# Two edits to a state-space and PReLU kernel: the last output blocks turned by TensorE, and a copy of the first group moved

## Chip, cores, metric

The kernel runs on one core of a Trainium2 chip. The metric is device time in microseconds (us), taken from repeated executions; a profile of one execution comes with it.

Names in the profile: PE is TensorE (PEld its weight loads), DVE is VectorE, ACT is ScalarE, POOL is GpSimd, SP is SyncE, which here only issues transfers and waits; a q behind a name is that engine's instruction queue. PSUM is the memory, in banks, that takes TensorE's products. A semaphore is a counter on which an engine waits.

## The reference, cut to what matters

```python
# x (4,8,768,32), a (4,8,768), B and C (4,8,768,16): a state-space layer, in chunks of 32
y = ssd(x, a, B, C)                          # state decays by a, output C . state
h = y.transpose(0, 2, 1, 3).reshape(3072, 256)
g = h @ w_in                                 # 256 -> 2048
g = max(g, 0) + alpha * min(g, 0)            # a slope per hidden unit
out = g @ w_out                              # 2048 -> 256, all in fp32
```

## The kernel before, the parts concerned

The 3072 tokens go in six groups of 512. Group 0 has plain products. The other groups use a scheme of seven products of half-size blocks in place of eight (as in Strassen's method), so that sums on VectorE and GpSimd, and copies on ScalarE, stand for one product in eight on TensorE. The seven results of a group lie in half banks of PSUM. From them `combine` makes two blocks `c[0]` and `c[1]` of 128 output columns by 512 tokens. They stand the wrong way round (columns on partitions), so `turn` turns them in 32x32 blocks on VectorE and stores pieces of 32 columns.

```python
def output(f, half=None):                    # group 0, second matrix
    ...
    if f == NF - 1 and half:                 # the last product of group 0
        for i, po in enumerate(pos.pop(0)):
            o_sb = op.tile([P, 2, d_model], F32, name="o_sb")
            nc.scalar.copy(out=o_sb, in_=po)             # L543
            nc.sync.dma_start(out=out[...], in_=o_sb)    # L545

HALVES = {1: (0, 0), 2: (0, 1), 7: (1, 0), 6: (1, 1), 3: (2, 0), 4: (2, 1), 5: (3, 0)}
#         product: (bank, half)

def combine(g):                              # cut; the branches of the last group
    nc.scalar.copy(out=sa[:, 0], in_=m[1])
    nc.vector.tensor_tensor(out=c[0][:, 0], in0=m[2], in1=sa[:, 0], op=ALU.add)
    turn(g, 0, c[0], slice(0, HT), engs)
    nc.scalar.copy(out=sa[:, 1], in_=m[5])
    nc.vector.tensor_tensor(out=u[:, 0], in0=m[6], in1=sa[:, 0], op=ALU.add)      # L687
    nc.vector.tensor_tensor(out=u[:, 1], in0=m[7], in1=u[:, 0], op=ALU.add)
    nc.vector.tensor_tensor(out=u[:, 0], in0=u[:, 0], in1=sa[:, 1], op=ALU.add)   # L690
    nc.gpsimd.tensor_tensor(out=c[1][:, 1], in0=u[:, 1], in1=sa[:, 1], op=ALU.add)
    nc.vector.tensor_tensor(out=c[1][:, 0], in0=u[:, 1], in1=m[4], op=ALU.subtract)  # L693
    turn(g, 1, c[1], slice(0, GT), engs)
    nc.vector.tensor_tensor(out=c[0][:, 1], in0=m[3], in1=u[:, 0], op=ALU.add)
    turn(g, 0, c[0], slice(HT, GT), engs)

def turn(g, i, c, ts, engs):
    nc.vector.transpose(o[:, :n], c.rearrange("p h t -> p (h t)")[:, ts])   # 32x32 blocks
    for a4 in range(P // 32):                # four transfers, rows of 32 floats = 128 B
        engs[a4 % len(engs)].dma_start(out=..., in_=o[32 * a4 : 32 * a4 + 32, :n]...)

for n in (1, 2, 5, 6, 7, 4, 3):              # the very end: the seven last products,
    product(NG - 1, NZ - 1, n)
for _ in combine(NG - 1):                    # then everything else
    pass
```

Of the kernel before, what the change touches and what calls it, by code (L numbers as in the profile page):

```python
# [9 lines left out]
F32 = mybir.dt.float32  # L10
U32 = mybir.dt.uint32
U16 = mybir.dt.uint16
ALU = mybir.AluOpType
# [9 lines left out]
def kernel(  # L23
# [25 lines left out]
    nc = tc.nc  # L49
# [6 lines left out]
    P = 128  # L56
    Q = 128
# [5 lines left out]
    d_model, d_ff = moe_w_in.shape  # L63
    KC = d_model // P
    NF = d_ff // P
    GC = 4
    GT = GC * Q
    NG = NCH // GC
# [3 lines left out]
    NZ = NF // 4  # L72
    HM = d_model // 2
    HT = GT // 2
# [10 lines left out]
    wtp = ctx.enter_context(tc.tile_pool(name="wtp", bufs=2))  # L85
# [3 lines left out]
    one = ctx.enter_context(tc.tile_pool(name="one", bufs=1))  # L89
# [4 lines left out]
    op = ctx.enter_context(tc.tile_pool(name="op", bufs=3))  # L94
    dr = ctx.enter_context(tc.tile_pool(name="dr", bufs=1, space=bass.MemoryType.DRAM))
    ps_s = ctx.enter_context(tc.tile_pool(name="ps_s", bufs=2, space=PSUM))
    ps_h = ctx.enter_context(tc.tile_pool(name="ps_h", bufs=2, space=PSUM))
    ps_q = ctx.enter_context(tc.tile_pool(name="ps_q", bufs=1, space=PSUM))

    def bank(i):  # L100


        return ps_q.tile([P, 512], F32, name="bank", tag=f"q{i}")
# [104 lines left out]
    def convert(dst, src, sg, add=nc.gpsimd):  # L208
# [14 lines left out]
        else:  # L223
            for i in range(2):
# [8 lines left out]
    ident = const.tile([P, P], F32, name="ident")  # L233
# [3 lines left out]
                          in_=ident.unsqueeze(1).to_broadcast([P, H, Q]))  # L237
# [275 lines left out]
    pos = {}  # L513
# [17 lines left out]
    def output(f, half=None):  # L531

        if f == 0:
            pos[0] = [bank(i).rearrange("p (t m) -> p t m", t=2) for i in range(GC // 2)]
        gt = gts[0, f]
        for t in range(GC) if half is None else range(2 * half, 2 * half + 2):
            nc.tensor.matmul(pos[0][t // 2][:, t % 2], gt[:, t * Q : (t + 1) * Q], w_out[:, f],  # L537
                             start=(f == 0 and t % 2 == 0), stop=(f == NF - 1),
                             skip_group_check=True)
        if f == NF - 1 and half:  # L540
            for i, po in enumerate(pos.pop(0)):
                o_sb = op.tile([P, 2, d_model], F32, name="o_sb")
                nc.scalar.copy(out=o_sb, in_=po)  # L543
                t0 = 2 * i * Q
                nc.sync.dma_start(  # L545
                    out=out[t0 : t0 + 2 * Q, :].rearrange("(s p) m -> p s m", p=Q), in_=o_sb)



# [5 lines left out]
    def weight_sums(w, sums, q0, part):  # L555


        if not sums:
            sums.extend(wld.tile([P, NQ, P], F32, name=f"ws{i}", tag="raw") for i in range(3))
        qs = slice(q0, q0 + 4)  # L560
        a11, a12, a21, a22 = w[:, qs, 0, 0], w[:, qs, 0, 1], w[:, qs, 1, 0], w[:, qs, 1, 1]
        s1, s2, s4 = (t[:, qs] for t in sums)
        o, x0, x1, f = ((s1, a21, a22, ALU.add), (s2, s1, a11, ALU.subtract),
                        (s4, a12, s2, ALU.subtract), (a21, a11, a21, ALU.subtract))[part]
        nc.gpsimd.tensor_tensor(out=o, in0=x0, in1=x1, op=f)
# [13 lines left out]

    ms = {}  # L580
    HALVES = {1: (0, 0), 2: (0, 1), 7: (1, 0), 6: (1, 1), 3: (2, 0), 4: (2, 1), 5: (3, 0)}
    blocks = {}

    def product(g, z, n):

        if z == 0 and n == 1:
            ms[g] = [t.rearrange("p (h t) -> p h t", h=2)
                     for t in [bank(i) for i in range(3)] + m5_bank]
        i, h = HALVES[n]
        s1, s2, s4 = out_sums  # L590
        for p in range(2):
            q = 2 * z + p
            w = {1: wq[:, q, 0, 0], 2: wq[:, q, 1, 0], 3: s4[:, q], 4: wq[:, q, 1, 1],
                 5: s1[:, q], 6: s2[:, q], 7: wq[:, q, 0, 1]}[n]
            nc.tensor.matmul(ms[g][i][:, h], w, blocks[g, z][n][:, p],  # L595
                             start=(q == 0 and h == 0), stop=(q == NQ - 1),
                             skip_group_check=True)

    def prelu(o, h, z, i):
# [4 lines left out]
        for p in range(2):  # L604
            nc.vector.scalar_tensor_tensor(out=o[:, p], in0=h[:, p], scalar=s_mul[:, fs[p]],  # L605
                                           in1=o[:, p], op0=ALU.mult, op1=ALU.max)

    def quad(g, z, after):


# [58 lines left out]
    ends_of = {}  # L669

    def combine(g):


        m = {n: ms[g][i][:, h] for n, (i, h) in HALVES.items()}
        sa = wtp.tile([P, 2, HT], F32, name="sa", tag="wr")
        u = wtp.tile([P, 2, HT], F32, name="u", tag="wr")
        c = [one.tile([P, 2, HT], F32, name=f"c{i}") for i in range(2)]
        last = g == NG - 1
        engs = [nc.sync, nc.scalar]
        nc.scalar.copy(out=sa[:, 0], in_=m[1])  # L680
        nc.vector.tensor_tensor(out=c[0][:, 0], in0=m[2], in1=sa[:, 0], op=ALU.add)
        if last:
            turn(g, 0, c[0], slice(0, HT), engs)
        yield
        nc.scalar.copy(out=sa[:, 1], in_=m[5])
        yield
        nc.vector.tensor_tensor(out=u[:, 0], in0=m[6], in1=sa[:, 0], op=ALU.add)  # L687
        nc.vector.tensor_tensor(out=u[:, 1], in0=m[7], in1=u[:, 0], op=ALU.add)
        if last:
            nc.vector.tensor_tensor(out=u[:, 0], in0=u[:, 0], in1=sa[:, 1], op=ALU.add)  # L690
            nc.gpsimd.tensor_tensor(out=c[1][:, 1], in0=u[:, 1], in1=sa[:, 1], op=ALU.add)
        yield
        nc.vector.tensor_tensor(out=c[1][:, 0], in0=u[:, 1], in1=m[4], op=ALU.subtract)  # L693
        if last:
            turn(g, 1, c[1], slice(0, GT), engs)
        nc.vector.tensor_tensor(out=c[0][:, 1], in0=m[3], in1=u[:, 0], op=ALU.add)
        ms.pop(g)
        if last:
            turn(g, 0, c[0], slice(HT, GT), engs)
        else:  # L700
            nc.gpsimd.tensor_tensor(out=c[0][:, 1], in0=c[0][:, 1], in1=sa[:, 1], op=ALU.add)
            nc.gpsimd.tensor_tensor(out=c[1][:, 1], in0=u[:, 1], in1=sa[:, 1], op=ALU.add)
            ends_of[g] = c

    def turn(g, i, c, ts, engs):

        n = ts.stop - ts.start
        o = op.tile([P, GT], F32, name="o_sb")
        nc.vector.transpose(o[:, :n], c.rearrange("p h t -> p (h t)")[:, ts])
        for a4 in range(P // 32):  # L710
            m0 = i * HM + 32 * a4
            t0 = g * GT + ts.start
            engs[a4 % len(engs)].dma_start(
                out=out[t0 : t0 + n, m0 : m0 + 32].rearrange("(b r) c -> r b c", r=32),
                in_=o[32 * a4 : 32 * a4 + 32, :n].rearrange("r (b c) -> r b c", c=32))

    def finish(g, i):
        turn(g, i, ends_of[g][i], slice(0, GT), [nc.sync])
# [3 lines left out]
    def ssm(gp, stages=1):  # L722

        if gp not in pairs:
            pairs[gp] = pair(gp)
        for i in range(stages):
            next(pairs[gp], None)
# [19 lines left out]
    for n in range(2):  # L747
        for f in range(NF):
            i = (n * NF + f) // 2
# [40 lines left out]
    for i in range(NZ * (NG - 1)):  # L790
        g, z = divmod(NZ + i, NZ)
        nxt = 2 * g + 2

        def after(j, g=g, z=z, i=i, nxt=nxt):
            if i and j in places:
                product(*divmod(NZ + i - 1, NZ), places[j])
            if i == 0:
                if j in (3, 5, 8, 9):
                    output(NF - LAG + (j > 5), {3: 0, 5: 1, 8: 0, 9: 1}[j])
            for w, sums, q0, part in late_sums.get((i, j), ()):  # L800
                weight_sums(w, sums, q0, part)
            if g > 1 and z == 0 and j in (5, 9, 13, 14):
                if j == 5:
                    comb[0] = combine(g - 1)
                next(comb[0], None)
            if g > 1 and z == 1 and j in (10, 13):
                finish(g - 1, j // 13)
            if nxt < NP and (z, j) in steps:
                ssm(nxt + steps[z, j])
            if nxt < NP and (z, j) == (3, 7):  # L810
                token_sums(g + 1)
            ahead = nxt + {(1, 3): 1, (3, 8): 2}.get((z, j), NP)
            if ahead < NP:
                if ahead == 6:
                    rows_turn(1, held["pr"])
                bns[ahead] = pair_loads(ahead)

        comb = [None] if i == 0 else comb
        if z == 0 and nxt < NP:
            if nxt == 4:  # L820
                load_rows(1)
                held["pr"] = rows_scan(1)
                rows_out(1)
            load_pair(nxt + 1)
        if z == 2 and nxt + 2 < NP:
            load_pair(nxt + 2)
        quad(g, z, after)
    for n in (1, 2, 5, 6, 7, 4, 3):
        product(NG - 1, NZ - 1, n)
    for _ in combine(NG - 1):  # L830
        pass


# [28 lines left out]
```

## Time and profile before

| | before |
|---|---|
| device time, median (range) of the 3 runs known at the prediction | 404.32 us (404.29 to 404.81) |
| span of the profiled execution | 402.8 us |
| TensorE busy | 378.4 us, 94% |
| longest idle of TensorE's matmuls after 100 us | 1.72 us, at 114.28 |
| TensorE's last product ends | 396.59 us |
| eight stores flow, 384 KB | 398.7 to 400.97 us |
| last landing, program's end | 401.69, 402.8 us |

A line of the timeline reads: start, length, engine, source line, operation, output <- inputs, shapes, count, and in brackets the idle time of that engine just before with what ended it. Such times are those of one execution. The trace also records when each transfer counts up its semaphore, which is its landing.

### The profile page before, as it was taken

What the parts mean: (1) busy time and instruction counts of PE and PEld (TensorE: products, weight loads), DVE (VectorE), ACT (ScalarE), POOL (GpSimd) and SP (SyncE); (2) the same over time, 40 slices, a digit from 0 to 9 for tenths busy, and PEclk for the clock granted to TensorE, in tenths of its full rate; (3) what the DMA queues carried; (4) which work ended last, traced back from release to release, by engine and by line L of the source; (5) the groups of instructions that cost most, each with busy time, mean ns of one, the idle gap of its engine ahead of it and who ended that gap; (6) DMA issues with size and microseconds to landing.
All of it is one profiled execution on the core that took longest, in us unless ns stands there. A gap on an engine that the chain in (4) does not pass through costs nothing.

```text
span 402.8 us, 6008 instructions
## 1 busy us (share of the span) xinstructions
PE 378.4 (94%) x2131; PEld 294.5 (73%) x2131; DVE 255.4 (63%) x493; ACT 180.2 (45%) x409; POOL 192.6 (48%) x188
## 2 busy tenths in 40 slices
PE   5878979999989999999999999999999999999993
PEld 4454638778858867877868878868878868888883
DVE  5889895691775573675764685674586574355363
ACT  3574823522444534554445544434534534534540
POOL 3164674578174954462453471453471454355511
PEclk9999999999999999999999999999999999999998
DMA  8939997100591430100791100891100200003003
GB/s 208 243 113 223 306 189 160 40 20 0 93 206 52 96 75 2 52 0 2 111 194 35 54 1 2 126 185 29 53 2 4 50 0 2 0 0 55 1 2 52
DMA packets 124126, 30.58 MB, mean 76 GB/s; under 512 B 96880, under 2 KB 120000, under 8 KB 124096
## 3 DMA queue, kind: packets, MB, share of 16 engines
q1 hardware_dynamic: 117792, 29.67, 33.2%
q10 hardware_dynamic: 6304, 0.52, 1.1%
q8 instruction: 17, 0.28, 0.3%
q14 instruction: 13, 0.11, 0.1%
HBM read 26.85 MB, written 3.34 MB: 75 GB/s over the span
## 4 chain that ended last, share of the span: by engine, by line
PE 81%; DVE 9%; ACT 3%; POOL 3%; issue 1%; DMA 1%; DVEq 0%; ACTq 0%; POOLq 0%
PE hp L620 30%; PE bank L595 29%; PE bank L537 6%; PE ss L478 5%; PE hp L524 4%; DVE dec L373 2%; PE ss L501 2%; ACT gt L603 1%; DVE wr L227 1%; DVE dec L483 1%; PE ss L407 1%; PE ss L447 1%; DVE gt L528 1%; POOL gt L663 1%; PE ss L494 1%
## 5 line engine op out<-in xcount | busy, mean ns | idle before, releaser
L663 POOL TENSOR_TENSOR gt<-gt 128x512 f32<-128x512 f32 x58 | 73.6, 1269 | 29.5 <-DVE gt L605 12.8
L595 PE MATMUL bank<-gt,w_out 128*128 128x256 f32 x320 | 82.1, 380 | 0.0
L605 DVE SCALAR_TENSOR_TENSOR gt<-hp,s_mul,gt 128x256 f32<-128x256 f32 x120 | 51.8, 477 | 44.8 <-ACT gt L603 41.7
L603 ACT ACTIVATE gt<-hp,s_alpha 128x256 f32<-128x256 f32 x120 | 50.0, 469 | 62.6 <-PE hp L620 61.3
L595 PEld LDWEIGHTS bank<-gt,w_out 128*128 128x128 f32 x320 | 60.3, 190 | 11.3 <-issue 2.3
L595 PE MATMUL bank<-gt,ws 128*128 128x256 f32 x240 | 58.9, 381 | 0.0
L654 POOL TENSOR_TENSOR gt<-gt 128x512 f32<-128x512 f32 x20 | 25.4, 1270 | 64.4 <-DVE gt L605 64.4
L595 PEld LDWEIGHTS bank<-gt,ws 128*128 128x128 f32 x240 | 45.2, 190 | 6.7 <-issue 0.8
L620 PE MATMUL hp<-xs,w_in 128*128 128x256 f32 x160 | 43.6, 395 | 0.5
L620 PE MATMUL hp<-xT,w_in 128*128 128x256 f32 x160 | 41.5, 382 | 1.7 <-DVE gt L605 1.7
L620 PE MATMUL hp<-xs,ws 128*128 128x256 f32 x160 | 42.3, 387 | 0.0
L379 DVE TENSOR_TENSOR_SCAN dec<-abc,bank 128x256 f32<-128x256 f32 x64 | 39.0, 665 | 0.0
L620 PEld LDWEIGHTS hp<-xs,w_in 128*128 128x128 f32 x160 | 28.1, 189 | 11.9 <-issue 5.9
L620 PEld LDWEIGHTS hp<-xs,ws 128*128 128x128 f32 x160 | 29.1, 190 | 10.1 <-issue 3.7
L620 PEld LDWEIGHTS hp<-xT,w_in 128*128 128x128 f32 x160 | 29.7, 190 | 6.7 <-DVE gt L605 3.1
L483 DVE TENSOR_TENSOR dec<-ss,dec 128x512 f32<-128x512 f32 x40 | 25.6, 682 | 10.5 <-PE ss L478 10.5
L605 DVE SCALAR_TENSOR_TENSOR gt<-c,s_mul,gt 128x256 f32<-128x256 f32 x40 | 17.7, 483 | 23.0 <-ACT gt L603 23.0
L537 PE MATMUL bank<-w_out,gt 128*128 128x256 f32 x128 | 30.4, 379 | 0.0
L524 PE MATMUL hp<-xT,w_in 128*128 128x256 f32 x96 | 25.7, 390 | 4.4 <-DVE gt L528 4.4
L639 DVE TENSOR_TENSOR hp<-hp,u 128x512 f32<-128x512 f32 x20 | 14.0, 700 | 21.7 <-ACT u L637 21.4
L537 PEld LDWEIGHTS bank<-w_out,gt 128*128 128x128 f32 x128 | 24.3, 190 | 3.3
L462 POOL TENSOR_TENSOR sm<-state,bmask 128x256 f32<-128x256 f32 (+1 forms) x12 | 7.7, 643 | 39.1 <-DVE state L458 39.1
(122 smaller groups left out, 539.0 us busy)
## 6 DMA issues: line engine op xcount, KB each, us to landing
abc<-z SPq DMA_DIRECT2D x20, 512.0 KB
raw<-in_moe_w_in_dram SPq DMA_DIRECT2D x8, 512.0 KB
raw<-in_moe_w_out_dram SPq DMA_DIRECT2D x8, 512.0 KB
xt<-in_x_dram SPq DMA_DIRECT2D x24, 128.0 KB
out_dram<-o_sb SPq DMA_DIRECT2D x34, 64.0 KB
nat<-in_B_dram SPq DMA_DIRECT2D x22, 64.0 KB
nat<-in_C_dram SPq DMA_DIRECT2D x22, 64.0 KB
ap<-pf SPq DMA_DIRECT2D x10, 128.0 KB
```

Source lines behind the costliest of these rows:

```text
L379: nc.vector.tensor_tensor_scan(out=dv[:, k, hs], data0=abc[k][:, hs], data1=ident_p[0], initial=0.0, op0=ALU.mult, op1=ALU.add)
L478: nc.tensor.matmul(gram[r].rearrange("p h t -> p (h t)"), bh[rs, k], cz[rs, :, k], start=True, stop=True, tile_position=(64 * r, 0), skip_ ...
L483: nc.vector.tensor_tensor(out=dec[:, k, hs], in0=gram[r], in1=dec[:, k, hs], op=ALU.mult)
L524: nc.tensor.matmul(hp, w_in[:, k, f * P : (f + 1) * P], xts[g][:, k, t0 : t0 + nt], start=(k == 0), stop=(k == KC - 1))
L537: nc.tensor.matmul(pos[0][t // 2][:, t % 2], gt[:, t * Q : (t + 1) * Q], w_out[:, f], start=(f == 0 and t % 2 == 0), stop=(f == NF - 1), s ...
L595: nc.tensor.matmul(ms[g][i][:, h], w, blocks[g, z][n][:, p], start=(q == 0 and h == 0), stop=(q == NQ - 1), skip_group_check=True)
L603: nc.scalar.mul(o[:, p], h[:, p], s_alpha[:, fs[p]])
L605: nc.vector.scalar_tensor_tensor(out=o[:, p], in0=h[:, p], scalar=s_mul[:, fs[p]], in1=o[:, p], op0=ALU.mult, op1=ALU.max)
L620: nc.tensor.matmul(to[:, p], w(2 * z + p), b, start=start and p == 0, stop=True, skip_group_check=True)
L639: nc.vector.tensor_tensor(out=Y, in0=Y, in1=u2, op=ALU.add)
L654: nc.gpsimd.tensor_tensor(out=tc_, in0=g22, in1=g12, op=ALU.subtract)
L663: eng.tensor_tensor(out=o, in0=x0, in1=x1, op=ALU.subtract)
```

## The change

Two places are meant to get shorter. At the end, TensorE has nothing left to do, so it turns whole 128x128 blocks in place of VectorE; each block is stored by one transfer with rows of 512 B; the fourth product moves to the fifth's bank so that it can be read while the third is being written; and each sum stands right behind the product it needs. In the middle, the copy of group 0's outputs waits until ScalarE has done what TensorE is waiting for.

```diff
-        if f == NF - 1 and half:
-            for i, po in enumerate(pos.pop(0)):
-                ...copy and store
+    def store_first():
+        for i, po in enumerate(pos.pop(0)):
+            ...copy and store
...
+    LAST = {**HALVES, 4: (3, 1)}
...
-        i, h = HALVES[n]
+        i, h = (LAST if g == NG - 1 else HALVES)[n]
...
+    def close(g):
+        def store(i, h, ps, copy, dma):
+            ps = ps.tile([P, 512], F32, name="turned", ...)
+            for b in range(2):
+                nc.tensor.transpose(ps[:, b * P : (b + 1) * P], c[i][:, h, b * P : (b + 1) * P],
+                                    ident)
+            o = op.tile([P, 2, HM], F32, name="o_sb")
+            copy(out=o.rearrange("p b m -> p (b m)"), in_=ps[:, :HT])
+            dma.dma_start(out=..., in_=o)
+        for n in (1, 2):
+            product(g, NZ - 1, n)
+        nc.scalar.copy(out=sa[:, 0], in_=m[1])
+        add(out=c[0][:, 0], in0=m[2], in1=sa[:, 0], op=ALU.add)
+        product(g, NZ - 1, 5)
+        nc.scalar.copy(out=sa[:, 1], in_=m[5])
+        turn(g, 0, c[0], slice(0, HT), [nc.sync, nc.scalar])
+        for n in (6, 7):
+            product(g, NZ - 1, n)
+        add(out=u[:, 0], in0=m[6], in1=sa[:, 0], op=ALU.add)
+        add(out=u[:, 1], in0=m[7], in1=u[:, 0], op=ALU.add)
+        nc.gpsimd.tensor_tensor(out=u[:, 0], in0=u[:, 0], in1=sa[:, 1], op=ALU.add)
+        add(out=c[1][:, 1], in0=u[:, 1], in1=sa[:, 1], op=ALU.add)
+        product(g, NZ - 1, 4)
+        add(out=c[1][:, 0], in0=u[:, 1], in1=m[4], op=ALU.subtract)
+        product(g, NZ - 1, 3)
+        store(1, 1, ps_h, nc.scalar.copy, nc.sync)
+        store(1, 0, ps_h, nc.scalar.copy, nc.scalar)
+        add(out=c[0][:, 1], in0=m[3], in1=u[:, 0], op=ALU.add)
+        store(0, 1, ps_s, nc.vector.tensor_copy, nc.sync)
...
-                    output(NF - LAG + (j > 5), {3: 0, 5: 1, 8: 0, 9: 1}[j])   # stored at (0, 9)
+            if (i, j) == (0, 13):
+                store_first()
```

More of the change, by code (lines that the diff above doesn't have):

```diff
@@ L539, in output @@
                              skip_group_check=True)
-        if f == NF - 1 and half:
-            for i, po in enumerate(pos.pop(0)):
-                o_sb = op.tile([P, 2, d_model], F32, name="o_sb")
-                nc.scalar.copy(out=o_sb, in_=po)
-                t0 = 2 * i * Q
-                nc.sync.dma_start(
-                    out=out[t0 : t0 + 2 * Q, :].rearrange("(s p) m -> p s m", p=Q), in_=o_sb)
+    def store_first():
+        for i, po in enumerate(pos.pop(0)):
+            o_sb = op.tile([P, 2, d_model], F32, name="o_sb")
+            nc.scalar.copy(out=o_sb, in_=po)
+            t0 = 2 * i * Q
+            nc.sync.dma_start(
+                out=out[t0 : t0 + 2 * Q, :].rearrange("(s p) m -> p s m", p=Q), in_=o_sb)
     wq = w_out.rearrange("p (q j) (i m) -> p q j i m", j=2, i=2)
@@ L677, in combine @@
         c = [one.tile([P, 2, HT], F32, name=f"c{i}") for i in range(2)]
-        last = g == NG - 1
-        engs = [nc.sync, nc.scalar]
         nc.scalar.copy(out=sa[:, 0], in_=m[1])
         nc.vector.tensor_tensor(out=c[0][:, 0], in0=m[2], in1=sa[:, 0], op=ALU.add)
-        if last:
-            turn(g, 0, c[0], slice(0, HT), engs)
         yield
@@ L688, in combine @@
         nc.vector.tensor_tensor(out=u[:, 1], in0=m[7], in1=u[:, 0], op=ALU.add)
-        if last:
-            nc.vector.tensor_tensor(out=u[:, 0], in0=u[:, 0], in1=sa[:, 1], op=ALU.add)
-            nc.gpsimd.tensor_tensor(out=c[1][:, 1], in0=u[:, 1], in1=sa[:, 1], op=ALU.add)
         yield
         nc.vector.tensor_tensor(out=c[1][:, 0], in0=u[:, 1], in1=m[4], op=ALU.subtract)
-        if last:
-            turn(g, 1, c[1], slice(0, GT), engs)
         nc.vector.tensor_tensor(out=c[0][:, 1], in0=m[3], in1=u[:, 0], op=ALU.add)
@@ L697, in combine @@
         ms.pop(g)
-        if last:
-            turn(g, 0, c[0], slice(HT, GT), engs)
-        else:
-            nc.gpsimd.tensor_tensor(out=c[0][:, 1], in0=c[0][:, 1], in1=sa[:, 1], op=ALU.add)
-            nc.gpsimd.tensor_tensor(out=c[1][:, 1], in0=u[:, 1], in1=sa[:, 1], op=ALU.add)
-            ends_of[g] = c
+        nc.gpsimd.tensor_tensor(out=c[0][:, 1], in0=c[0][:, 1], in1=sa[:, 1], op=ALU.add)
+        nc.gpsimd.tensor_tensor(out=c[1][:, 1], in0=u[:, 1], in1=sa[:, 1], op=ALU.add)
+        ends_of[g] = c
@@ new lines, in close @@
+    def close(g):
+        m = {n: ms[g][i][:, h] for n, (i, h) in LAST.items()}
+        sa = wtp.tile([P, 2, HT], F32, name="sa", tag="wr")
+        u = wtp.tile([P, 2, HT], F32, name="u", tag="wr")
+        c = [one.tile([P, 2, HT], F32, name=f"c{i}") for i in range(2)]
+        add = nc.vector.tensor_tensor
+        def store(i, h, ps, copy, dma):
+            ps = ps.tile([P, 512], F32, name="turned", tag="hp" if ps is ps_h else "ss")
+            for b in range(2):
[3 more added lines that the diff above has]
+            copy(out=o.rearrange("p b m -> p (b m)"), in_=ps[:, :HT])
+            t0 = g * GT + h * HT
+            dma.dma_start(out=out[t0 : t0 + HT, i * HM : (i + 1) * HM]
+                          .rearrange("(b p) m -> p b m", p=P), in_=o)
+        for n in (1, 2):
[18 more added lines that the diff above has]
+        store(0, 1, ps_s, nc.vector.tensor_copy, nc.sync)
@@ L827 @@
         quad(g, z, after)
-    for n in (1, 2, 5, 6, 7, 4, 3):
-        product(NG - 1, NZ - 1, n)
-    for _ in combine(NG - 1):
-        pass
+    close(NG - 1)
 _INS = ['x', 'a', 'B', 'C', 'moe_w_in', 'moe_w_out', 'moe_alpha']
```

## The prediction

> **What bounds the kernel now.** I read the page's busy shares and its chain first, to see which engine sets the time.
>
> ```profile
> PE 378.4 (94%) x2131; PEld 294.5 (73%) x2131; DVE 255.4 (63%) x493; ACT 180.2 (45%) x409; POOL 192.6 (48%) x188
> ...
> PE 81%; DVE 9%; ACT 3%; POOL 3%; issue 1%; DMA 1%; DVEq 0%; ACTq 0%; POOLq 0%
> ```
>
> TensorE (PE) is busy 94% of the 402.8 us and carries 81% of the chain. The change adds six small TensorE instructions and takes none away. It can therefore gain only where TensorE stands idle: in a hole in the middle, or after its last product. So I looked for the idle times of TensorE's matmuls. After 100 us there are two: 1.72 us at 114.28 and 0.99 us at 156.73. The first lies where the copies of the first group stand, so I took the chain of waits around it (start us, length us, what):
>
> ```profile
> 110.79 0.84 ACT gt L603 x2
> 111.63 0.95 ACT o_sb L543 x2
> 112.58 0.04 ACT gt L603
> 112.61 0.23 issue
> 112.84 0.49 ACT gt L603
> 113.33 0.02 issue
> 113.35 0.89 DVE gt L605 x2
> 114.24 0.04 issue
> ```
>
> Before TensorE can go on it needs the buffer `hp`, which VectorE (DVE, L605) frees after ScalarE (ACT, L603). Ahead of that L603 ScalarE copies two finished output banks (L543, 0.95 us), which nobody in the chain needs. The timeline of the same time tells when the others were free:
>
> ```profile
> 110.57 1.13 PE L620 MATMUL hp<-xs,w_in 128*128 128x256 f32 x4
> ...
> 111.54 1.03 PE L620 MATMUL hp<-xT,w_in 128*128 128x256 f32 x4
> 112.06 0.72 DVE L458 SCALAR_TENSOR_TENSOR state<-state,ap,ss 128x128 f32<-128x128 f32 x2
> ...
> 113.35 1.66 DVE L605 SCALAR_TENSOR_TENSOR gt<-hp,s_mul,gt 128x256 f32<-128x256 f32 x4 [0.57 <-ACT gt L603]
> ```
>
> The input of L603 was in PSUM at 110.57 + 1.13 = 111.70, and VectorE was free at 112.78, 0.57 us before it got its work.
>
> The other place is the end. The timeline from 396 us (TensorE's last product ends at 396.59 by the chain):
>
> ```profile
> 395.88 0.42 DVE L690 TENSOR_TENSOR u<-u,sa 128x256 f32<-128x256 f32 x1
> 395.92 0.97 POOL L691 TENSOR_TENSOR c<-u,sa 128x256 f32<-128x256 f32 x1 [2.38 <-DVE u L688]
> ...
> 396.62 0.42 DVE L693 TENSOR_TENSOR c<-u,bank 128x256 f32<-128x256 f32 x1 [0.32 <-PE bank L595]
> 397.13 0.71 DVE L709 STREAM_TRANSPOSE o_sb<-c 128x512 f32<-128x512 f32 x1
> 397.77 0.39 DVE L696 TENSOR_TENSOR c<-bank,u 128x256 f32<-128x256 f32 x1
> 397.87 1.92 SPq L713 DMA_DIRECT2D out_dram<-o_sb  x4
> 397.87 2.02 ACTq L713 DMA_DIRECT2D out_dram<-o_sb  x4
> 398.19 0.45 DVE L709 STREAM_TRANSPOSE o_sb<-c 128x256 f32<-128x256 f32 x1
> ```
>
> VectorE works alone: subtract, turn, add, turn. L693 needs only the fourth product (done one product, 0.86 us, before the third), yet it waits for TensorE until 396.59, because the fourth shares its bank with the third. Then eight transfers are issued, four on each of two queues. Busy time by stretch (last columns: PEclk, DMA share, GB/s) shows when their data move:
>
> ```profile
> 398.40:398.70 0.30, 0.00 (x0) 0.00 (x0) 0.23 (x1) 0.00 (x0) 0.00 (x0) 1.00 0.00 0
> 398.70:400.00 1.30, 0.00 (x0) 0.00 (x0) 0.00 (x0) 0.00 (x0) 0.00 (x0) 0.72 1.05 175
> 400.00:400.90 0.90, 0.00 (x0) 0.00 (x0) 0.00 (x0) 0.00 (x0) 0.00 (x0) 0.50 1.19 183
> 400.90:402.80 1.90, 0.00 (x0) 0.00 (x0) 0.00 (x0) 0.00 (x0) 0.00 (x0) 0.50 0.01 1
> ```
>
> The first issue starts at 397.87 and data flow from about 398.73, 0.86 us later. The transfers then run without a gap for 2.2 us at some 180 GB/s with the DMA engines full, and 1.9 us follow in which nothing moves until the span ends. From the last product to the end: 402.8 - 396.59 = 6.2 us.
>
> **What the Trainium skill says.** "DMA: Bandwidth & Descriptors", section Specifications, asks for at least 512 B per piece for line rate; below it DMA does a read-modify-write. The view of transfers counts 4288 of the 4289 packets of the last 13 us under 512 B (the stores' rows of 32 floats, 128 B), and 180 GB/s with full engines agrees: at 112.5 to 114, with larger packets, they moved 346 to 376 GB/s. The same page, section Anatomy of one DMA, lays most of a transfer's fixed cost on the receipt of the last write; the 1.9 us of silence agree, and no store can avoid them. "VectorE: DVE Perf Modes", section The three transpose paths: VectorE turns 32x32 blocks only, TensorE a full 128x128 but into PSUM, so a copy is needed after. The 128 B rows are the mark of the first; copies are in the change. "SBUF — State Buffer", section Who interferes with whom: a VectorE instruction with two SBUF inputs shuts GpSimd's reads out. L691 beside L690 took 0.97 us, where the same size alone (L577) takes 0.73 to 0.74; this agrees.
>
> **Part 1: the first group's copies three places later.** The order of the built kernel confirms that on ScalarE the two copies now stand after the four L603, nothing else moving there. L603 can start at 111.70 + 0.04 = 111.74 (before: 112.47) and takes 0.84, so ends 112.58. VectorE, in its order, first does L458 until 112.78, so L605 starts at 112.80 instead of 113.35 and TensorE at 113.73 instead of 114.28: 0.55 us. The next buffer comes free when ScalarE has done the other pair (after TensorE's 111.54 + 1.03 = 112.57: to 113.45) and VectorE too (113.68 to 114.56), 0.05 to 0.1 us after TensorE would want it. I count **0.5 us**. The copies (0.95 to 1.05 us, to some 114.5) end before ScalarE's next input, then at about 114.9. The banks they read are written again only in the next block (117.27 before), and TensorE has no other such idle until 156.73, which moves along: the gain stays.
>
> **Part 2: the end,** on the clock of before. The fourth product goes to the bank of the fifth; the products still end at 396.59.
> - u on GpSimd beside VectorE's add, as L691 was beside L690: ends 396.89. VectorE: 395.88 to 396.30, then without the wait for the third product 396.34 to 396.76.
> - TensorE turns the two c[1] blocks from 396.6 and 396.8. One turn (L407) lasts 0.27 us and four follow each other at 0.11, so a pair is 0.38 plus the load of 0.14. ScalarE copies (0.37 as L411) end at some 397.4 and 397.75; each store is issued then, one on each queue.
> - The last block: add after u, 396.93 to 397.33; pair of turns to about 397.85; VectorE's copy (0.42, as L426 that also reads PSUM) to 398.30; one issue at 398.32; flow from + 0.86 = 399.18; 128 KB in 512 B rows at 350 GB/s (an estimate from the rate above) 0.37: 399.55; silence 1.9: **401.45**. Before it was 402.8: **1.35 us**.
> - So two VectorE turns (0.71 and 0.45 us) and eight issues of some 0.45 us, four in a row on each queue, give way to three pairs of turns, three copies and three issues. The earlier two stores flow from about 398.3 and 398.65, and so are out of the way.
>
> Sum 0.5 + 1.35 = 1.85 us; 404.32 - 1.85 = 402.47, and I say **402.4 us**.
>
> **Rivals.** (a) *The silence is the bound and the stores were hidden anyway*: the end gains only what the last issue gains. The last issue started at about 399.4 before and starts at 398.3 after, 1.1 us, and the flow's tail shrinks; so at least 0.8 us. Total 1.3: 403.0. (b) *GpSimd becomes the bound of the end*: u now lies on the path. If GpSimd starts first, VectorE is the one shut out, and both the turned blocks and the last add come 0.4 us later: 402.9. Against it: VectorE started 0.04 us earlier before. (c) *The copies only change victim*: later copies delay the next block's ScalarE or, through the later store, the loads queued behind it on SP: 0.5 lost, 403.0; the loads are for two blocks ahead, which speaks against it. (d) *Larger packets gain more than I say*, 512 B stores landing sooner: 402.0.
>
> **Range and chances.** Repeats of the kernel before spread 0.5 us (404.29 to 404.81), (a) to (d) 402.0 to 403.0; so 401.7 to 403.2. Two per cent are 8.1 us, more than the whole 6.2 us after the last product plus the hole of 1.7 us: faster by over 2% has 1%, slower 0.5%.
>
> **What would show it.** Right: the idle of 1.72 us becomes about 1.2; the subtraction of the fourth product starts before TensorE's last product ends; span about 401; the last packets 512 B, and no stretch of 2 us with full DMA engines at the end; 1.9 us of silence still there. Wrong: the hole keeps 1.7 us or another opens before 156 us; GpSimd's add takes over 1.2 us; the turns take over 0.8 us a pair; the silence changes by more than 0.3 us.

## The result and the profile after

The changed kernel took 401.82 us (median of 4 runs, 401.6 to 403.0) against 404.56 us before (median of 4, 404.29 to 404.95). The ratio is 0.9937, with a 95% interval of 0.9916 to 0.9959; it is the mean time of one kernel's fast runs over that of the other's fast runs of the same rounds, so not quite the ratio of these medians. That is 2.55 us of 404.56; by the interval it can be 1.7 to 3.4 us, so timing alone does not tell the gain from the 1.9 us that were forecast. The interval lies wholly below 1. The time lies in the predicted range, at its fast end.

In the timeline after, around the idle in the middle (L606 and L608 are what L603 and L605 were before):

```profile
111.29 1.76 ACT L606 ACTIVATE gt<-hp,s_alpha 128x256 f32<-128x256 f32 x4
...
112.25 1.70 DVE L608 SCALAR_TENSOR_TENSOR gt<-hp,s_mul,gt 128x256 f32<-128x256 f32 x4
...
113.18 1.13 PE L623 MATMUL hp<-xT,w_in 128*128 128x256 f32 x4 [1.07 <-DVE gt L608]
```

ScalarE now runs its four activations without a break, and TensorE's idle went from 1.72 to 1.07 us. In the timeline after, at the end:

```profile
394.84 0.97 POOL L727 TENSOR_TENSOR u<-u,sa 128x256 f32<-128x256 f32 x1 [2.38 <-DVE u L726]
395.14 0.41 DVE L730 TENSOR_TENSOR c<-u,bank 128x256 f32<-128x256 f32 x1
...
395.85 0.42 DVE L734 TENSOR_TENSOR c<-bank,u 128x256 f32<-128x256 f32 x1 [0.29 <-POOL u L727]
396.15 1.49 SPq L713 DMA_DIRECT2D out_dram<-o_sb  x2
396.32 0.20 PEld L708 LDWEIGHTS turned<-ident,c 128*128 128x128 f32 x2 [0.52 <-DVE c L734]
396.32 0.44 PE L708 MATMUL turned<-ident,c 128*128 128x128 f32 x2 [0.28 <-DVE c L734]
...
396.80 0.42 DVE L711 COPY o_sb<-turned 128x256 f32<-128x256 f32 x1 [0.53 <-PE turned L708]
```

The fourth product is subtracted (L730) without waiting for the third. The last block waits for GpSimd (L734), then goes through turn, copy and store one after the other. The busy times by stretch after show the transfers (the last two columns are DMA share and GB/s):

```profile
397.10:398.00 0.90, 0.00 (x0) 0.00 (x0) 0.12 (x1) 0.00 (x0) 0.00 (x0) 1.00 0.96 285
398.00:398.10 0.10, 0.00 (x0) 0.00 (x0) 0.00 (x0) 0.00 (x0) 0.00 (x0) 1.00 0.00 0
398.10:398.70 0.60, 0.00 (x0) 0.00 (x0) 0.00 (x0) 0.00 (x0) 0.00 (x0) 1.00 0.73 219
398.70:399.90 1.20, 0.00 (x0) 0.00 (x0) 0.00 (x0) 0.00 (x0) 0.00 (x0) 1.00 0.00 0
```

There is no long jam any more: the first two stores flow for 0.9 us, there is a gap, and the last flows alone. And the silence at the end (from the last data packet to the end of the span), 1.9 us before, is only 1.2 us. To see what it is made of, I looked at the program's own closing instructions (count, durations in ns, first and last start). Before, then after:

```profile
L857 SPq EVENT_SEMAPHORE  x7: 17/28/28, 401.7 to 402.7; - x7
L857 SPq DRAIN  x3: 7/7/13, 402.0 to 402.4; - x3
```

```profile
L888 SPq EVENT_SEMAPHORE  x7: 17/28/28, 397.7 to 399.8; - x7
L888 SPq DRAIN  x3: 7/7/13, 399.1 to 399.4; - x3
```

SP waits for the transfers' eight semaphores in five instructions of a fixed order, about 0.07 us apart where nothing is left to wait for; a DRAIN instruction follows them. Before, the first wait got through at 401.7, right after the last landing (401.69), and the other four had to follow. After, four of them had been passed by 398.4 and only the last held, until the landing at 399.04.

For a comparison that one slow load or a throttle cannot blur, I cut each trace at two points: TensorE's first matmul, and the start of VectorE's sum of the sixth product (L687 before, L725 after; 394.89 and 393.81 us). The first matmul comes after the first loads and varies from run to run (4.43 to 5.01 us), with no relation to the edits; in the trace after it was 0.46 us earlier than before, and that part of the two spans' difference (2.9 us) is not the change's.

| stretch, us | before | after | difference |
|---|---|---|---|
| first matmul to sum of the sixth product | 390.00 | 389.38 | -0.62 |
| that sum to the last data packet | 6.08 | 4.88 | -1.20 |
| last data packet to last landing | 0.72 | 0.36 | -0.36 |
| last landing to SP's drain | 0.35 | 0.08 | -0.27 |
| drain to the end | 0.76 | 0.76 | 0 |
| sum | 397.91 | 395.45 (by unrounded values 395.46) | -2.45 |

The 2.45 us of the stretches lie well inside the interval of the timed 2.55 us.

The 1.20 us up to the last data packet are mostly the last issue, which stands 1.10 us earlier (4.54 us after the sum of the sixth product before, 3.44 after). Before, VectorE had turned the last block at 398.64, but its last transfer, the fourth in a row on ScalarE's queue, was issued only at 399.43, 0.79 us later; after, the issue follows the end of the copy by 0.03 us. So by these two traces some 0.76 us come from issuing fewer transfers in a row, and 0.34 us from having the block ready sooner. No run tests the two apart.

### The profile page after: what moved, and what is told of

Same layout as the page of the kernel before. It is cut to its first block, busy times and chain, and to the rows that moved or that the text cites. A ratio compares the mean times of both kernels' runs of the same rounds, so it can differ in the third digit from the quotient of the medians.

```text
span 399.9 us, 6018 instructions
## 1 busy us (share of the span) xinstructions
PE 378.9 (95%) x2137; PEld 295.0 (74%) x2137; DVE 254.6 (64%) x492; ACT 181.5 (45%) x411; POOL 192.8 (48%) x188
## 4 chain that ended last, share of the span: by engine, by line
PE 81%; DVE 10%; ACT 3%; POOL 3%; issue 1%; DMA 1%; POOLq 0%; DVEq 0%; ACTq 0%
PE hp L623 31%; PE bank L598 28%; PE bank L537 6%; PE ss L478 5%; PE hp L524 4%; DVE dec L373 2%; PE ss L501 2%; DVE wr L227 1%; DVE dec L483 1%; ACT gt L606 1%; PE ss L407 1%; PE ss L447 1%; DVE gt L528 1%; POOL gt L666 1%; PE ss L494 1%
## 5 line engine op out<-in xcount | busy, mean ns | idle before, releaser
L608 DVE SCALAR_TENSOR_TENSOR gt<-hp,s_mul,gt 128x256 f32<-128x256 f32 x120 | 51.9, 477 | 44.2 <-ACT gt L606 41.2
L606 ACT ACTIVATE gt<-hp,s_alpha 128x256 f32<-128x256 f32 x120 | 50.2, 469 | 62.7 <-PE hp L623 61.2
L608 DVE SCALAR_TENSOR_TENSOR gt<-c,s_mul,gt 128x256 f32<-128x256 f32 x40 | 17.7, 483 | 23.0 <-ACT gt L606 23.0
```

The lines of the kernel that those rows point to most:

```text
L606: nc.scalar.mul(o[:, p], h[:, p], s_alpha[:, fs[p]])
L608: nc.vector.scalar_tensor_tensor(out=o[:, p], in0=h[:, p], scalar=s_mul[:, fs[p]], in1=o[:, p], op0=ALU.mult, op1=ALU.max)
```

## The experiments

Each run is correct unless said otherwise. The times scatter more than the effects. In this table "clock in the trace" is the mean of TensorE's granted clock in the profiled execution. In some executions the trace shows it at half speed for 3.4 or 6.8 us at a time before 60 us (in the run with the late copies alone from 51.5 to 58.4 us). In the four rows under 0.99 the first stretch is longer for this, by 0.65 to 1.4 us, all of it lost by 61 us. The 0.996 of the kernel before is another thing: there the half speed begins at 399.27 us, when TensorE has nothing more to do. So I read the stretches first and the timed ratios second. The stretches repeat well: without such a loss the first is 390.00 or 390.01 us in four traces with the early copies and 389.34 to 389.38 us in five with the late ones.

| run | clock in the trace | to the sum of the sixth | from there to the end | packet to landing | landing to drain | timed ratio to before, 95% interval |
|---|---|---|---|---|---|---|
| before | 0.996 | 390.00 | 7.91 | 0.72 | 0.35 | |
| after | 1.000 | 389.38 | 6.07 | 0.36 | 0.08 | 0.9937 (0.9916 to 0.9959) |
| copies late alone | 0.988 | 390.01 | 7.91 | 0.71 | 0.35 | 0.9973 (0.9958 to 0.9989) |
| new end alone | 1.000 | 390.01 | 6.06 | 0.35 | 0.08 | 0.9930 (0.9917 to 0.9942) |
| bank alone | 0.996 | 390.00 | 7.96 | 0.70 | 0.35 | 0.9985 (0.9970 to 0.9999) |
| after, four loads more | 0.985 | 390.39 | 6.32 | 0.35 | 0.34 | 0.9938 (0.9923 to 0.9953) |
| before, four loads more | 0.995 | 390.01 | 7.64 | 0.72 | 0.08 | 0.9983 (0.9964 to 1.0003) |
| after, pieces of 128 B | 0.998 | 389.36 | 6.80 | 0.54 | 0.08 | 0.9953 (0.9931 to 0.9976) |
| after, one store more | 0.996 | 389.38 | 7.74 | 0.35 | 0.19 | one look |
| after, bank back | 1.000 | 389.35 | 7.10 | 0.35 | 0.08 | 0.9951 (0.9932 to 0.9970) |
| after, idle filled | 0.999 | 388.47 | 6.07 | 0.35 | 0.08 | 0.9905 (0.9879 to 0.9930) |
| after, additions changed over | 0.985 | 390.41 | 6.81 | 0.35 | 0.08 | 0.9957 (0.9933 to 0.9981) |
| after, last copy in halves | 0.996 | 389.34 | 6.19 | 0.35 | 0.08 | 0.9935 (0.9912 to 0.9958) |
| filled, additions changed over | 0.987 | 389.85 | 6.09 | 0.35 | 0.08 | 0.9900 (0.9883 to 0.9917) |

### The two parts one at a time

The late copies alone, on the kernel before:

```diff
-        if f == NF - 1 and half:
-            ...copy and store
+            if (i, j) == (0, 13):
+                store_first()
```

> The kernel before with the later copies of the first group alone. My theory, from the two traces: the two parts do not touch each other, and TensorE's idle of 1.72 us near 114 us falls to 1.07 us, so the time falls by 0.65 us (the prediction said 0.5) and the stretch from VectorE's sum of the sixth product to the end of the span stays at 7.91 us. Rival: the copies only change their victim; then the idle falls but another opens before 160 us and the time stays within 0.2 us. Rival: the 0.46 us by which the whole trace after was ahead from its first matmul on belong to the change; then this kernel or the next is ahead by it at its first matmul too.

The new end alone is the changed kernel with that edit undone.

> The changed kernel with the first group's copies back at their old place, so the new end alone. My theory: the idle near 114 us is 1.72 us as before, and the stretch from VectorE's sum of the sixth product to the end of the span falls from 7.91 to 6.1 us, so the time falls by 1.8 us (the prediction said 1.35), with a silence after the last data packet of 1.2 to 1.3 us instead of 1.9. Rival: the short silence was luck of one profile; then it is 1.9 us here and the time falls by 1.2 to 1.35 us.

TensorE's line after the idle, with the late copies alone, then with the new end alone:

```profile
114.28 1.13 PE L621 MATMUL hp<-xT,w_in 128*128 128x256 f32 x4 [1.06 <-DVE gt L606]
```

```profile
114.35 1.13 PE L622 MATMUL hp<-xT,w_in 128*128 128x256 f32 x4 [1.72 <-DVE gt L607]
```

The parts do not touch each other. The copies shorten the idle to 1.06 us and leave the end at 7.91 us; from the product before the last one of the block to the first of the next block it is 3.06 us (111.22 to 114.28), and 3.71 before (110.57 to 114.28). The whole stretch hides this, because this trace had 6.8 us at half clock earlier. From 114.28 us to the sum of the sixth product both traces take 280.6 us, so no other idle took its place. The new end leaves the idle and shortens the end to 6.06 us; the short silence was no luck. Neither trace is ahead at its first matmul (4.89 and 4.94 us), so the 0.46 us are not the change's. The timed -0.7% of the new end alone (2.8 us) is more than the 1.85 us of its stretches: its runs had clocks of 0.995 to 1, those of before in the same rounds 0.98 to 0.996.

### The bank alone, and the bank undone

On the kernel before, the last group's products and `combine` use the new placement, in the old order:

```diff
+    LAST = {**HALVES, 4: (3, 1)}
-        i, h = HALVES[n]
+        i, h = (LAST if g == NG - 1 else HALVES)[n]
```

> The kernel before with the fourth product of the last group in the fifth's bank, and nothing else. My theory: the subtraction of the fourth product starts right after VectorE's add at 396.30 instead of 396.62, but the turn of both c1 blocks that follows needs GpSimd's add, which ends at 396.89, so it starts at about 396.93 instead of 397.13 and everything behind it is 0.2 us earlier: the time falls by 0.2 us. Rival: the bank carries most of the gain, since a whole product of 0.86 us need not be waited for: the time falls by 0.6 to 0.9 us.

Neither theory was right: the end is 7.96 us, 0.05 us later. The timeline of this run:

```profile
395.30 0.37 ACT L686 COPY sa<-bank 128x256 f32<-128x256 f32 x1 [3.08 <-DMA out_dram<-o_sb]
395.70 0.42 DVE L691 TENSOR_TENSOR u<-u,sa 128x256 f32<-128x256 f32 x1 [0.38 <-ACT sa L686]
```

A new wait took the place of the old one. In the old order the copy of the fifth product (L686) stands behind all seven products, and it now waits until the fourth, its new neighbour in the bank, has been written: it starts at 395.30, 0.87 us after the sum of the sixth product, where before it started 0.33 us ahead of it. VectorE's next addition waits for the copy. The line puts the wait down to a transfer; the built program has this copy wait for TensorE alone, and the next product began at 395.10 with the fourth in front of it, so I take it to be TensorE.

The other way round, in the changed kernel:

```diff
-    LAST = {**HALVES, 4: (3, 1)}
+    LAST = HALVES
```

> The changed kernel with the fourth product back in the third's bank, everything else as changed. My theory: with the new order of the program (subtract the fourth, then compute the third) TensorE must now wait with the third product until VectorE has read the fourth, which it does until about 1.75 us after its sum of the sixth product; the third product then ends some 0.9 us later than before and the end comes 0.6 to 0.7 us later than in the changed kernel. Rival: the bank is worth nothing, as it was when it was moved alone; the end stays where it is (within 0.1 us).

```profile
395.92 1.13 PE L598 MATMUL bank<-gt,ws 128*128 128x256 f32 x4 [0.97 <-DVE c L730]
```

TensorE stands idle before the third product until VectorE has read the fourth, and the end is 1.03 us later, more than I expected. So the bank and the order belong together: the bank without the order gains nothing, the order without the bank costs 1.03 us of the 1.84.

### What the silence at the end is made of

Four loads of 8 KB that nobody uses, some 80 us before the end, shift the last store by four in the round of eight semaphores.

```diff
+            if (i, j) == (16, 1):
+                spare = one.tile([NF, 4, P], F32, name="spare")
+                for r in range(4):
+                    nc.sync.dma_start(out=spare[:, r],
+                                      in_=moe_alpha.rearrange("(k p) -> k p", p=P))
```

In the changed kernel:

> The changed kernel with four loads of 8 KB that nobody uses, issued some 80 us before the end where SP is idle. They move the last store on by four in the round of eight semaphores, from the one that the program's closing waits ask for last to one that they ask for first. My theory: part of the silence at the end is those closing waits, five in a fixed order of 0.07 us each; with the last landing in the first of them the other four are still to come, so from the last landing to the drain that follows the waits it takes 0.35 us instead of 0.08, and the time rises by 0.27 us. Rival: the silence is the receipt of the last write alone, and nothing changes (within 0.1 us).

In the kernel before:

> The kernel before with the four unused small loads, the mirror of the run with them in the changed kernel. My theory: its last store now counts on the semaphore that the closing waits ask for last; from the last landing to the drain it takes 0.08 us instead of 0.35, the receipt stays at 0.72 us, and the stretch from VectorE's sum of the sixth product to the end falls from 7.91 to 7.64 us. Rival: the order of those waits is not what decides; no change.

Both came out. Landing to drain went from 0.08 to 0.34 us in the one and from 0.35 to 0.08 us in the other, and the ends moved by 0.25 and 0.27 us. The closing instructions of the changed kernel with the loads:

```profile
L893 SPq EVENT_SEMAPHORE  x7: 17/28/28, 400.6 to 401.6; - x7
L893 SPq DRAIN  x3: 7/7/13, 401.0 to 401.3; - x3
```

The first wait gets through at 400.6 (the last landing is at 400.62) and the drain comes 0.34 us later, as in the kernel before. So 0.27 us of the gain are an accident of how many transfers the program has: the change issues five fewer at its end, and the last one fell on a semaphore asked for last. Timed, 0.27 us cannot be told from nothing here (0.9983, 0.9964 to 1.0003).

For the receipt, two of the three last stores were given pieces of 128 B. The result is wrong on purpose.

```diff
+            if h == 1:
+                o = op.tile([P, 8, 64], F32, name="o_sb")
+                copy(out=o[:, :, :32], in_=ps[:, :HT].rearrange("p (j c) -> p j c", c=32))
+                dma.dma_start(out=out[t0 + i * P : t0 + (i + 1) * P, :]
+                              .rearrange("p (j c) -> p j c", c=32), in_=o[:, :, :32])
+                return
```

> The changed kernel with the first and the last of its three final stores in pieces of 128 B instead of 512 B, still one transfer of 128 KB each and at the same times (the result is wrong on purpose: the two blocks land in other rows). Moving the last 128 KB should take 0.7 us at the 180 GB/s of the kernel before, instead of 0.5. Theory A: short pieces make the last receipt long; then the time from the last data packet to the last landing rises from 0.36 to about 0.7 us as in the kernel before, and the end is 0.55 us later in all. Theory B: in the kernel before the receipt was long because eight transfers had been queued behind each other; then it stays at 0.35 to 0.45 us and the end is 0.2 to 0.3 us later.

This did not separate the theories: 0.54 us lies between them. The stores of 1024 pieces started to flow 1.27 and 1.25 us after their issue instead of 0.9, so that all three ran into one flow of 1.8 us. The result was wrong, with a relative error of 0.29. So the next run makes a long flow of long pieces:

```diff
         store(1, 1, ps_h, nc.scalar.copy, nc.sync)
+        waste = dr.tile([H, P, Q], F32, name="waste")
+        nc.sync.dma_start(out=waste.rearrange("e p c -> p e c"),
+                          in_=ident_h.rearrange("p (e c) -> p e c", e=H))
```

> The changed kernel with one more store of 512 KB, in pieces of 512 B, to memory that nobody reads, issued between the first and the last of the three final stores on the same queue. The data then flow without a gap for about 2.5 to 3 us at 340 GB/s, as long as the 2.26 us of the kernel before, but in pieces of 512 B. Theory A: the late last receipt of the kernel before (0.72 us after the last data packet) comes from its pieces of 128 B; then it stays at 0.35 to 0.4 us here. Theory B: it comes from the queue of writes behind each other; then it rises to 0.6 us or more.

```profile
397.30:400.40 3.10, 0.00 (x0) 0.00 (x0) 0.13 (x1) 0.00 (x0) 0.00 (x0) 0.70 1.01 294
400.40:400.50 0.10, 0.00 (x0) 0.00 (x0) 0.00 (x0) 0.00 (x0) 0.00 (x0) 0.50 0.06 15
```

Data flowed without a gap for 3.2 us, longer than before, and the last landing came 0.35 us after the last packet. So a long flow of 512 B pieces did not make the receipt late; in these runs only flows with 128 B pieces did. (This is one look, with four stores in 1792 pieces; the kernel before has eight in 3072. That the number of pieces or of stores decides, and not their size, is not tested.) A long flow belongs to it too: the four small stores of 128 B pieces that both kernels issue near 394 us flow for only 1.0 us and land 0.39 to 0.43 us after their last packet. With pieces of 128 B the traces thus show 0.4, 0.54 and 0.72 us after flows of 1.0, 1.8 and 2.26 us (the second with some long pieces in it). Inside the long flow of the kernel before one sees it grow: its eight stores, in the order of their last packets, land 0.34, 0.37, 0.45, 0.49, 0.56, 0.69, 0.70 and 0.72 us after them. Stores in pieces of 512 B need 0.34 to 0.39 us in every trace, and 0.43 us where one flows among short pieces. Why it grows so is open. (The 0.19 us from landing to drain in this run fit too: one transfer more puts the last store on another semaphore.)

### What still holds the middle and the end

The remaining idle of 1.07 us: the first Gram pair of the next state-space block (two products of C with B on TensorE) moved into it.

```diff
+        ahead_gram = gp == 2 * GC // 2
+        if ahead_gram:
+            grams(0)
+            yield
...
+            if (i, j) == (0, 12):
+                ssm(nxt)
```

> The changed kernel with two of TensorE's products (the first Gram pair of the next state-space block, 1.06 us) moved 2 us ahead into the idle of 1.07 us that is left near 113 us; VectorE's two multiplications of them (1.29 us) move along. My theory: that idle is a chain of ScalarE and VectorE that nothing on TensorE can shorten, so work moved into it is free: the idle falls under 0.3 us and the stretch from the first matmul to VectorE's sum of the sixth product falls by 0.8 to 1.0 us against the changed kernel, 3.2 to 3.5 us in all against the kernel before. Rival: VectorE's 1.29 us come too early and push the scans behind them, another idle of TensorE opens before 125 us, and less than 0.3 us is gained.

```profile
112.19 1.53 PE L472 MATMUL ss<-cz,bh 64*128 64x512 f32 x4
```

No idle is left, and the stretch falls by 0.91 us. So 0.9 of the pair's 1.06 us went into the idle and cost nothing: TensorE had been waiting there for ScalarE and VectorE.

At the end, GpSimd's addition was taken off the last block's path:

```diff
-        nc.gpsimd.tensor_tensor(out=u[:, 0], in0=u[:, 0], in1=sa[:, 1], op=ALU.add)
-        add(out=c[1][:, 1], in0=u[:, 1], in1=sa[:, 1], op=ALU.add)
+        add(out=u[:, 0], in0=u[:, 0], in1=sa[:, 1], op=ALU.add)
+        nc.gpsimd.tensor_tensor(out=c[1][:, 1], in0=u[:, 1], in1=sa[:, 1], op=ALU.add)
...
-        store(1, 1, ps_h, nc.scalar.copy, nc.sync)
         store(1, 0, ps_h, nc.scalar.copy, nc.scalar)
+        store(1, 1, ps_h, nc.scalar.copy, nc.sync)
```

> The changed kernel with two additions at the end changed over: VectorE adds the fifth product to u, GpSimd makes the block c1 from it, and the stores of the two c1 blocks change places. My theory: in the changed kernel GpSimd's add (0.97 us beside VectorE's) ends 2.0 us after the sum of the sixth product and holds the last block up; without it the last add starts when VectorE is free, at about 1.75 instead of 2.04, and the turn of the last block follows the turn of GpSimd's block at about 2.25 instead of 2.5: the end is 0.2 to 0.25 us earlier (6.07 to 5.85 us). Rival: the third product or TensorE's turns were the bound and GpSimd was only beside them; no gain (within 0.05 us).

```profile
398.52 0.37 ACT L711 COPY o_sb<-turned 128x256 f32<-128x256 f32 x1 [0.60 <-PE turned L708]
398.92 0.90 SPq L713 DMA_DIRECT2D out_dram<-o_sb  x2
```

The last block's copy did start 0.25 us earlier (2.74 us after the sum of the sixth product instead of 2.99), so GpSimd was on the path. But the end came 0.74 us later. I had given ScalarE a store to issue between its two copies; the second copy had to wait for that issue, and the last block's store stood behind that copy's store in SP's queue. A mistake of mine in the experiment, but a real trap.

The last copy in halves:

```diff
-        store(0, 1, ps_s, nc.vector.tensor_copy, nc.sync)
+        for b, (ps, copy) in enumerate(((ps_s, nc.vector.tensor_copy), (ps_h, nc.scalar.copy))):
+            ps = ps.tile([P, 512], F32, name="turned", ...)
+            nc.tensor.transpose(ps[:, :P], c[0][:, 1, b * P : (b + 1) * P], ident)
+            copy(out=o[:, b], in_=ps[:, :P])
+        nc.sync.dma_start(...)
```

> The changed kernel with the last block's copy out of PSUM cut into halves in two banks, one by VectorE and one by ScalarE at the same time, still one store. My theory: every step of the last block is on the path, so a copy of 0.27 us (as ScalarE's copies of this half size) instead of 0.42 makes the end 0.1 to 0.15 us earlier. Rival: the end is set by the transfers that are already flowing, not by the last block; no gain.

```profile
397.12 0.27 ACT L740 COPY o_sb<-turned 128x128 f32<-128x128 f32 x1 [0.62 <-PE turned L739]
```

It cost 0.12 us. The turned halves were there at 396.81 by the timeline, and VectorE began its half at 396.74, but ScalarE was issuing a store from 396.54 to 396.94 and began only at 397.12. Both theories missed that.

Last, the filled idle and the changed additions together, with the stores so placed that no issue or queue stands in the way:

> The changed kernel with the products that fill the idle, and with the two additions changed over between VectorE and GpSimd; the stores now so that no queue holds a late store up: the first c1 block on SP, GpSimd's block on ScalarE's queue, the last block on SP. My theory: the stretch to VectorE's sum of the sixth product is that of the filling run (388.5 us); the last block's copy ends 0.25 us earlier, as it did in the run with the additions changed over, and this time its store follows at once, so the end falls from 6.07 to about 5.8 us; with the same clock the span is about 1.15 us shorter than the changed kernel's and 3.6 us shorter than the kernel before. Rival: the end gains nothing for another reason that the late store hid; then 0.9 us alone are left.

```profile
397.21 0.92 SPq L719 DMA_DIRECT2D out_dram<-o_sb  x2
```

The middle keeps its gain; the timed ratio is 0.9900. (The stretch of 389.85 us is from a trace with half clock early on; no idle of TensorE is left near 113 us in it.) But the end did not move: 6.09 us. The last store was issued at 397.74, 3.20 us after the sum of the sixth product instead of 3.44, and its last packet still came 4.90 us after it, as in the changed kernel (4.88). Both c1 blocks are stored later now (2.67 and 2.95 us after that sum instead of 2.34 and 2.68), so the three stores stand close together and flow as one, 384 KB from 398.11 to 399.44, with a DMA share of 1.06 from 398.2 to 399.4. The wait was for GpSimd; it became one for the DMA engines. The simpler version with only the idle filled, 0.9905, does as well. By its stretches it is 0.9 us ahead of the changed kernel; the timed intervals of the two overlap.

## Why the prediction was right, and where its size was off

- **What bounds the kernel, and where a gain can be**: right. Only the idle near 114 us and the end changed.
- **The idle in the middle, 0.5 us**: the mechanism was right, the size a little small: 0.65 us by the idle, 0.62 by the stretch. VectorE began L608 at 112.25, 0.08 us before the end by the timeline of the work in front of it, where I had it begin 0.02 us after; and TensorE did not wait for the second buffer at all (0.97 us between the two first steps of the next block, before and after), where I took off 0.05 to 0.1. The prediction's own numbers spoke against that: 113.73 + 0.97 = 114.70 is later than the 114.56 at which it had the buffer free.
- **The end up to the last issue**: right to 0.02 us. From the start of the sum of the sixth product, in us, as predicted and as measured: GpSimd's add ends 2.00 and 2.00; last add ends 2.44 and 2.46; pair of turns 2.96 and 2.95; copy 3.41 and 3.41; issue 3.43 and 3.44; data begin to flow 4.29 and 4.33. (The copies of the two c1 blocks ended some 0.2 us sooner than worked out, 2.64 instead of 2.86 for the second; nothing on the path waited for them.)
- **The flow of the last 128 KB, 0.37 us**: too small, 0.55 us. It ramps up and down (82, 271, 353, 343, 231 and 31 GB/s in tenths of a microsecond), and the 350 GB/s I took were those of a longer run of transfers.
- **The silence of 1.9 us, "no store can avoid them"**: this is the step that failed, the one large mis-sized term. It was 1.20 us. I had read one number as one fixed cost and given it to the receipt. By the last packet it was 1.83 us before, and it has three parts: the receipt, 0.72 us before and 0.36 after, which was late only in flows with short pieces; closing waits in a fixed order, 0.35 and 0.08 us, which depend on which semaphore is last; and 0.75 to 0.76 us that are the same in all 14 traces. So the 1.9 us did not agree with a cost that is mostly receipt, as the prediction said. The prediction named a change of the silence by more than 0.3 us as a sign of being wrong, and that sign showed.
- **In sum**: 1.85 us were worked out and 2.45 us are in the stretches. The end gained 1.84 instead of 1.35 (-0.70 silence, +0.18 flow, +0.04 start of the flow), the middle 0.62 instead of 0.5. That the time still lay in the range is in part luck: 0.27 us of it are the accident of the semaphores, the short flow took 0.18 us back, and the range reached so far down for a reason of its own, rival (d).
- **The rivals**: (a), that the end gains only what the last issue gains, fell: that was 1.10 us, as it said, and the end gained 1.84. That the copies only change victim (c) fell with their run alone. That GpSimd becomes the bound of the end (b) was half right, since it holds up the last block by 0.29 us, though not by more than I had put into the sum. That larger pieces gain more than I say (d) came true in small part: the receipt was 0.36 us shorter, but the last flow 0.18 us longer than I had it. That its estimate of 402.0 was nearer to the outcome than mine is luck as well, since the semaphores and the middle made up the rest.
- **The bank**: the prediction counted it as a wait removed and no more. The runs show that alone it gains nothing, and that in the new order it is worth 1.03 us.

## What to carry to other kernels

Look for the gain where the busiest engine stands idle, and follow the instructions of the engine that it waits for in their order: work nobody waits for, ahead of work somebody waits for, is the cheapest thing to move, and an idle that a chain leaves over can take other work. A bank of PSUM and the order of the instructions have to be changed together, since in these runs a wait was put on everything issued so far in that bank. Count the transfers that stand in a row on each queue at the end, since each issue took 0.3 to 0.5 us in both kernels. Take the silence after the last store apart into receipt, closing waits and constant before calling it fixed, and keep stores to be issued off an engine whose next copy is on the path.

## What the Trainium skill lacked or had wrong

- "DMA: Bandwidth & Descriptors", section Anatomy of one DMA, gives a fixed cost of about 2 us that scales with nothing, most of it the receipt (fitted for another issuing path than SP and ScalarE). Here the receipt, last packet to landing, was 0.34 to 0.39 us with pieces of 512 B, even after 3.2 us of flow, and 0.34 to 0.72 us with pieces of 128 B, growing along a flow. It was the smaller part: 0.82 to 0.92 us passed from the first store's issue to its first data (1.27 with 1024 pieces).
- The same page, section Issuing engines are not separate DMA queues, calls the time that an issue takes on its sequencer usually small. Here an issue on ScalarE took 0.40 us and held back ScalarE's own next copy: 397.12 instead of about 396.8 us.
- No page was found that tells of the closing waits: SP asks for the transfers' semaphores in a fixed order, 0.07 us each, so that which semaphore the last store counts on moved the end by 0.25 to 0.27 us, and 0.75 to 0.76 us pass from there to the end in every run.
